# A drain written out by hand: eight pieces of an expert's first product, three routing groups, GpSimd for the W2 halves

## The chip, the core and the metric

The kernel runs on one core of a Trainium2 chip. TensorE (PE in the profile; PEld is its weight load), VectorE (DVE), ScalarE (ACT) and GpSimd (POOL) each run their own instruction list in order; SyncE (SP) issues most of the transfers, also in order. The metric is the device time of one execution in microseconds; lower is better.

## The reference, cut to what matters

Chunked attention (chunks of 64, 8 heads of 64) makes 4608 tokens of 512 numbers; each token then passes a mixture of eight experts, if its skip score is positive:

```python
scores = scale * np.matmul(q_c, k_c.transpose(0, 1, 2, 4, 3))
scores = scores - np.max(scores, axis=-1, keepdims=True)
attn = np.exp(scores)
attn = attn / (np.sum(attn, axis=-1, keepdims=True) + 1e-09)
out = np.matmul(attn, v_c)
...
do_compute = x @ w_skip > 0
e_idx = np.argmax(xc @ w_gate, axis=1)
for e in range(E):
    mask = e_idx == e
    h = np.maximum(xc[mask] @ w1[e], 0.0)
    y[mask] = gate_w[mask, None] * (h @ w2[e])
out[do_compute] = xc + y
```

`w1` is 8 x 512 x 1024, `w2` 8 x 1024 x 512.

## The kernel before, in words

**Tile loop (L605).** The tokens are 36 tiles of 128 (NT = 36). Iteration i works on several tiles at once: scores of tile i+1 (L211), their row maximum on VectorE (L216), its subtraction (L222), the exponential on ScalarE (L226), transposes of the probabilities (L233), product with v (L248), division into x (L258), transposes of x (L279), x split into two float16 parts `xh` (L290 on ScalarE, L292 and L293 on GpSimd; for the last three tiles L286 on ScalarE and L287 on VectorE), nine logits by eight small matmuls (L306, L307), and their reduction `lg` (L316). The loop runs to i = NT + 3, so its last four iterations hold only the tail of the last tiles.

**Routing.** Tiles are routed in groups, `GS = (14, 9, 7, 6)`. When a group's last logits are there, the generator `route` (L323) gives out small steps: kind "d" is VectorE work (maximum, exponent, comparisons `eh`, gate; later `ad`, `rank`, `bi`, `sl`, `key`, `ohb` and one one-hot `oh` per tile, L393, with a product `rv` on GpSimd, L392), kind "p" TensorE work (rank matmuls L363 to L366, record matmuls L410). `run_route` takes a few steps per iteration, up to a budget. After group 2 the first three blocks of 128 tokens of the first expert are known; they are gathered by GpSimd (L467), transposed and split into `xt0` (`early_xt`, L480 to L482).

**Weights.** The first expert's weights come in 16 halves (L453), W1 halves first. Each is split into two float16 parts: the high one on ScalarE (L459), the low one on GpSimd (L463, L464) or on VectorE (L461). The staging tiles `wst` have 8 buffers, which the next expert's loads (L573, four chunks of two halves ahead) share.

**Pieces.** `piece()` (L594) is one of eight chunks of the first product of those 384 tokens: 12 matmuls of 128x384 (L488) into one bank of an `sp` tile of two banks. `evac()` moves a finished one to `ht0`: L492 on ScalarE, L493 on VectorE. After the last routing group come the remaining gathers and the second product `y` (L517), with which the expert phase begins; from there on units of blocks follow each other.

**What sets the order.** The code is recorded in the order in which it is written, and each engine runs its part in order. A tile's buffer is written again once its readers are done, so a piece recorded after an `evac()` of the other bank of its `sp` tile waits for that `evac()`. The pools of the expert phase (`ps_h`, `ps_y`, `ps_x`) take the PSUM banks of the loop's pools, and `bpool` takes SBUF of the loop's pool, x tiles included.

Of the kernel before, what the change touches and what calls it, by code (L numbers as in the profile page):

```python
# [18 lines left out]
P = 128  # L19
# [4 lines left out]
DM = H * D  # L24
# [13 lines left out]
GS = (14, 9, 7, 6)  # L38
# [10 lines left out]
W_TILES = (23, 24, 25, 26, 27, 28, 29, 30, 33, 33, 34, 34, 35, 35, 36, 36)  # L49
# [8 lines left out]
EARLY_AT = {EARLY_I: 0, EARLY_I + 1: 1, EARLY_I + 2: 2}  # L58
# [39 lines left out]
def moe_attention_kernel(ctx: ExitStack, tc: tile.TileContext, q: bass.AP, k: bass.AP, v: bass.AP, cst: bass.AP, wall: bass.AP, out: bass.AP):  # L98
# [167 lines left out]
    def stores(i):  # L266
        if 0 <= i - 3 < STORED:
            store(i - 3)
        elif STORED <= i - 3 < NT:
            held.append(i - 3)  # L270
        for _ in range(4 if i > NT - 4 else 0):
            if held:
                store(held.pop(0))

    def pe_xtrans(t):
        x = T[t].pop("x")
        xt = ps_p.tile([P, KC, P], F32, name="xt")
        for j in range(KC):
            nc.tensor.transpose(xt[:, j, :], x[:, j * P:(j + 1) * P], ident)  # L279
        T[t]["xt"] = xt  # L280
# [42 lines left out]
    def route(g):  # L323
# [66 lines left out]
        for i in range(n):  # L390
            yield "d", 200
            nc.gpsimd.tensor_tensor(rv[:, i], ohb[:, i].unsqueeze(1).to_broadcast([P, 4, NB]), vt[:, i, :].unsqueeze(2).to_broadcast([P, 4, NB]), op=ALU.mult)  # L392
# [212 lines left out]
    for i in range(-1, NT + 4):  # L605
# [7 lines left out]
        if i > NT:  # L613
            piece()
# [14 lines left out]
        run_route("d", 900 if i < NT - 1 else 1500)  # L629
        if i in EARLY_AT:  # L630
            early_xt(EARLY_AT[i], xt_bank if i < NT else sp_bank)
# [5 lines left out]
        if w_pend and (len(w_pend) > 1 or W_TILES[FC - 1] < i < W_TILES[FC]):  # L637
            if i < W_TILES[FC]:
                conv_half()
# [6 lines left out]
        if i >= NT:  # L646
            for eng in (nc.vector, nc.gpsimd):
                if w_pend:
                    conv_half(eng)
            evac()  # L650
        if i == NT:
            piece()
            piece()
# [3 lines left out]
    while routes:  # L657
        host.clear()
        run_route("w", 1)
        piece()  # L660
        run_route("p", 1)
        run_route("rd", 1 << 30)
        evac()
# [3 lines left out]
    while todo or evs:  # L667
        evac()
        piece()
# [4 lines left out]
    ps_h = ctx.enter_context(tc.tile_pool(name="ps_h", bufs=3, space=PSUM))  # L674
    ps_y = ctx.enter_context(tc.tile_pool(name="ps_y", bufs=3, space=PSUM))
    ps_x = ctx.enter_context(tc.tile_pool(name="ps_x", bufs=2, space=PSUM))
# [202 lines left out]
```

## Time and profile before

| | us |
|---|---|
| three runs: median (lowest to highest) | 386.1 (384.02 to 386.74) |
| the profiled execution | 388.72 |
| its span, first to last instruction | 387.0 |

The profiled execution is 2.6 us above the median of the runs, and 1.7 us of it lie outside its span. Times in the rows count from the span's start. The profile has a page (busy shares, a strip of 40 slices, the chain of work that ended last) and answers about stretches of the trace. In a timeline row, the first number is the start and the second the duration; "x12" is the number of instructions merged, and "[1.49 <-DVE ht L493]" is idle time of the engine before them with what ended it.

### The profile page before, as it was taken

Reading aid. Unit: us, or ns where it says so; the run is one execution under the profiler, and the core shown is the slowest. Engines: PE = TensorE matmul, PEld = TensorE weight load, DVE = VectorE, ACT = ScalarE, POOL = GpSimd, SP = SyncE. Lnnn points to the kernel's source line nnn. Section 1 sums busy time; section 2 is a strip of 40 time slices with the busy share of each in tenths; the row PEclk is TensorE's granted clock in tenths of the full one; section 3 lists DMA queues with packets and bytes.
Section 4 is the critical chain, followed back from the end, with each engine's and each line's share of the span. In section 5 each row is a group of like instructions: output and inputs, shape, how many; then the busy total and the mean of one; then the engine's idle time right before and its main releaser. Section 6 shows DMA issues by size and latency. Waiting matters only on the chain.

```text
span 387.0 us, 11298 instructions
## 1 busy us (share of the span) xinstructions
PE 328.2 (85%) x4544; PEld 230.0 (59%) x4544; DVE 250.7 (65%) x575; ACT 164.9 (43%) x336; POOL 148.0 (38%) x200
## 2 busy tenths in 40 slices
PE   6777777788776796767699999899999999999992
PEld 3666766677675674433346554476575665859570
DVE  1555545699679668136555599978597686876520
ACT  3344343445654342221514475445465454654320
POOL 5155444478899844034522002512411324011110
PEclk9999989999999876886999999999999999999998
DMA  8999798899988940222547067776747867665000
GB/s 274 392 368 326 242 331 258 274 304 319 337 262 278 323 163 29 81 75 90 142 176 219 3 216 250 238 254 218 249 149 221 269 208 251 206 201 184 29 24 26
DMA packets 42472, 81.83 MB, mean 211 GB/s; under 512 B 5150, under 2 KB 5150, under 8 KB 42416
## 3 DMA queue, kind: packets, MB, share of 16 engines
q1 hardware_dynamic: 39168, 71.47, 55.7%
q0 software_dynamic: 3104, 9.33, 7.9%
q8 instruction: 37, 0.61, 0.7%
q10 hardware_dynamic: 144, 0.26, 0.2%
q14 instruction: 19, 0.16, 0.1%
HBM read 67.01 MB, written 14.17 MB: 210 GB/s over the span
## 4 chain that ended last, share of the span: by engine, by line
PE 69%; DVE 14%; issue 7%; ACT 5%; DMA 3%; POOLq 0%; POOL 0%; ACTq 0%; DVEq 0%
PE y L517 25%; PE hp L488 19%; PE sp L488 5%; PE sp L211 4%; PE xt L279 4%; PE pv L248 4%; DVE oh L393 3%; ACT xs L290 3%; DMA qk<-in_k 2%; PE xq L480 2%; PE xt L306 2%; DVE mx L216 1%; PE pt L233 1%; DVE ht L493 1%; PE sp L222 1%
## 5 line engine op out<-in xcount | busy, mean ns | idle before, releaser
L517 PE MATMUL y<-wset,ht 128*128 128x512 f16 (+7 forms) x552 | 101.9, 379 | 1.2 <-DVE ht L493 1.2
L488 PEld LDWEIGHTS <-wset 128*128 128x128 f16 x864 | 76.0, 101 | 36.4 <-issue 18.4
L488 PE MATMUL hp<-xt,wset 128*128 128x288 f16 (+6 forms) x768 | 81.1, 267 | 1.7 <-DVE ht L493 1.1
L467 POOL DMA_INDIRECT out<-yo,reci x22 | 24.5, 1111 | 146.4 <-DVE yo L527 125.2
L517 PEld LDWEIGHTS <-ht 128*128 128x128 f16 (+7 forms) x552 | 45.7, 101 | 47.7 <-issue 3.4
L691 DVE SCALAR_TENSOR_TENSOR wset<-wst,wset 128x512 f16<-128x512 f32 x112 | 71.5, 683 | 1.4 <-ACT wset L690 0.8
L690 ACT ACTIVATE wset<-wst 128x512 f16<-128x512 f32 x112 | 63.0, 621 | 2.6 <-DMA wst<-in_wall 2.6
L492 ACT ACTIVATE ht<-hp 128x288 f16<-128x288 f32 (+6 forms) x64 | 23.4, 371 | 50.2 <-PE hp L488 49.6
L290 ACT ACTIVATE xs<-xt 128x512 f32<-128x512 f32 x33 | 19.7, 596 | 58.8 <-PE xt L279 57.0
L216 DVE TENSOR_REDUCE mx<-sp 128x8 bf16<-128x512 f32 x36 | 24.7, 687 | 25.5 <-PE sp L211 23.9
L493 DVE SCALAR_TENSOR_TENSOR ht<-hp,ht 128x288 f16<-128x288 f32 (+6 forms) x64 | 25.3, 405 | 23.3 <-ACT ht L492 22.3
L293 POOL TENSOR_TENSOR xh<-xs,xh 128x512 f16<-128x512 f32 x33 | 38.2, 1158 | 2.6
L292 POOL CAST xh<-xs 128x512 f16<-128x512 f32 x33 | 20.4, 617 | 45.3 <-ACT xs L290 45.1
L248 PE MATMUL pv<-v,pts 64*64 64x65 f32 x1152 | 28.6, 229 | 9.5 <-issue 9.0
L211 PE MATMUL sp<-qk 64*64 64x64 f32 x1152 | 27.1, 230 | 6.1 <-issue 4.7
L248 PEld LDWEIGHTS pv<-v,pts 64*64 64x64 f32 x1152 | 23.8, 142 | 11.4 <-issue 10.9
L488 PE MATMUL sp<-xt,wset 128*128 128x384 f16 x96 | 23.6, 418 | 7.1 <-DVE ht L493 6.3
L481 ACT ACTIVATE xt<-xq 128x512 f16<-128x512 f32 (+7 forms) x19 | 9.6, 509 | 42.3 <-PE xq L480 42.3
L279 PE MATMUL xt<-ident,x 128*128 128x128 f32 x144 | 24.9, 297 | 2.8 <-DVE xt L482 1.8
L467 POOL DMA_INDIRECT xg<-out,reci x22 | 24.2, 1101 | 7.3 <-issue 5.2
L211 PEld LDWEIGHTS sp<-qk 64*64 64x64 f32 x1152 | 21.5, 139 | 9.2 <-issue 7.7
L226 ACT ACTIVATE px<-sp 128x512 f32<-128x512 f32 x36 | 21.6, 600 | 11.4 <-PE sp L222 11.3
(118 smaller groups left out, 389.2 us busy)
## 6 DMA issues: line engine op xcount, KB each, us to landing
wst<-in_wall SPq DMA_DIRECT2D x128, 256.0 KB
v<-in_v SPq DMA_DIRECT2D x36, 260.0 KB
qk<-in_q SPq DMA_DIRECT2D x36, 256.0 KB
out<-x SPq DMA_DIRECT2D x36, 256.0 KB
qk<-in_k SPq DMA_DIRECT2D x35, 256.0 KB
xg<-out,reci POOLq DMA_INDIRECT x22, 4.5
out<-yo,reci POOLq DMA_INDIRECT x22, 4.6
qk<-in_k ACTq DMA_DIRECT2D x1, 256.0 KB
```

Of the source, the lines that this page charges most:

```text
L211: nc.tensor.matmul(sp[halves[a], c, j * CH:(j + 1) * CH], qk[halves[c], 0, w], qk[halves[c], 1, w], start=(j == 0), stop=False, skip_group ...
L216: nc.vector.tensor_reduce(mx, T[t]["sp"][:, :, :KC * CH].rearrange("p c (j s) -> p c j s", s=CH), axis=AX.X, op=ALU.max, negate=True)
L248: nc.tensor.matmul(pv[halves[c], jj, m * VW:(m + 1) * VW], pt[halves[jj], c * 2 + jp, halves[a]], vv[halves[jj], c * KC + m, :], start=(m ...
L279: nc.tensor.transpose(xt[:, j, :], x[:, j * P:(j + 1) * P], ident)
L290: nc.scalar.activation(xs, T[t].pop("xt"), AF.Copy, scale=SX)
L293: nc.gpsimd.tensor_tensor(xh[:, 1], xs, xh[:, 0], op=ALU.subtract)
L467: ins = nc.gpsimd.indirect_dma_start(**kw)
L488: nc.tensor.matmul(hp, w[:, a, fc, j * P:(j + 1) * P], xt[:, b, j, :n], start=(m == 0), stop=(m == 11))
L493: nc.vector.scalar_tensor_tensor(ht[:, 1, fc, :n], hp, 0.0, ht[:, 0, fc, :n], op0=ALU.max, op1=ALU.subtract)
L517: nc.tensor.matmul(y[c * P // cg:c * P // cg + n], ht[:, a, fc, o:o + n], w[:, b, fc, P * KC:], start=(f == 0 and m == 0), stop=(f == fw - ...
L690: nc.scalar.activation(w[:, 0, fc, r], st[part], AF.Copy, scale=SW)
L691: nc.vector.scalar_tensor_tensor(w[:, 1, fc, r], st[part], SW, w[:, 0, fc, r], op0=ALU.mult, op1=ALU.subtract)
```

## The change

The loop ends at i = NT - 1. What its last four iterations held, and the `while routes` loop behind it, becomes one straight list of calls. In it the pieces stand one by one: first piece, transposes of tile 34, logits of 33, evacuation, second piece, transposes of 35, logits of 34, evacuation, third piece, logits of 35, the first routing steps, evacuation, fourth piece, rank matmuls, fifth and sixth piece, record matmuls, seventh and eighth. `GS` becomes (14, 9, 13): groups 3 and 4 are one, routed wholly in the list. All W2 halves are split by ScalarE and GpSimd, one per iteration from i = 33 on and the last five in the list; in the last group GpSimd makes `rv` in two instructions of up to seven tiles. W2 loads are issued a little earlier, the third early block and the transposes of the last tiles use `sp` and `pt` banks, the "d" budget is 1100 instead of 900 from i = 27, and `ps_x` is placed before `ps_y`.

```diff
-GS = (14, 9, 7, 6)
+GS = (14, 9, 13)
-W_TILES = (23, 24, 25, 26, 27, 28, 29, 30, 33, 33, 34, 34, 35, 35, 36, 36)
+W_TILES = (23, 24, 25, 26, 27, 28, 29, 30, 32, 33, 33, 34, 34, 34, 35, 35)
-    def pe_xtrans(t):
+    def pe_xtrans(t, bank=None):
...
-            nc.gpsimd.tensor_tensor(rv[:, i], ohb[:, i].unsqueeze(1).to_broadcast([P, 4, NB]), vt[:, i, :].unsqueeze(2).to_broadcast([P, 4, NB]), op=ALU.mult)
+            s = slice(i, i + 1) if g + 1 < NG else slice(i, min(i + 7, n))
+            sv = [P, s.stop - i, 4, NB]
+            if g + 1 < NG or i % 7 == 0:
+                nc.gpsimd.tensor_tensor(rv[:, s], ohb[:, s].unsqueeze(2).to_broadcast(sv), vt[:, s, :].unsqueeze(3).to_broadcast(sv), op=ALU.mult)
...
-    for i in range(-1, NT + 4):
+    for i in range(-1, NT):
...
-        run_route("d", 900 if i < NT - 1 else 1500)
+        run_route("d", 900 if i < sum(GS[:EARLY_G]) + 4 else 1100)
...
-        if w_pend and (len(w_pend) > 1 or W_TILES[FC - 1] < i < W_TILES[FC]):
-            if i < W_TILES[FC]:
-                conv_half()
+        if w_pend and (i > W_TILES[FC] or i < W_TILES[FC] and (len(w_pend) > 1 or i > W_TILES[FC - 1])):
+            conv_half()
...
-        if i >= NT:
-            for eng in (nc.vector, nc.gpsimd):
-                if w_pend:
-                    conv_half(eng)
-            evac()
-        if i == NT:
-            piece()
-            piece()
     feed_load()
-    while routes:
...
+    pe_ptrans(NT - 1)
+    pe_xtrans(NT - 3, sp_bank)
+    ve_norm(NT - 2)
+    ac_pt(NT - 1)
...
+    ac_xs(NT - 3)
+    pe_logits(NT - 4)
+    ve_logits(NT - 4)
+    early_xt(EARLY_B - 1, sp_bank)
+    pe_pv(NT - 1)
+    ve_norm(NT - 1)
+    store(NT - 1)
+    feed_load()
+    conv()
+    piece()
+    pe_xtrans(NT - 2, pt_bank)
+    ac_xs(NT - 2)
+    pe_logits(NT - 3)
+    ve_logits(NT - 3)
+    evac()
+    conv()
+    piece()
+    pe_xtrans(NT - 1, pt_bank)
+    ac_xs(NT - 1)
+    pe_logits(NT - 2)
+    ve_logits(NT - 2)
+    evac()
+    conv()
+    piece()
+    pe_logits(NT - 1)
+    ve_logits(NT - 1)
+    run_route("d", 1 << 30)
+    evac()
+    conv()
+    piece()
+    run_route("p", 1)
+    run_route("rd", 1 << 30)
+    piece()
+    evac()
+    conv()
+    piece()
+    evac()
+    conv()
+    run_route("w", 1)
+    run_route("p", 1)
+    run_route("rd", 1 << 30)
...
     while todo or evs:
+        piece()
         evac()
-        piece()
...
+    ps_x = ctx.enter_context(tc.tile_pool(name="ps_x", bufs=2, space=PSUM))
     ps_y = ctx.enter_context(tc.tile_pool(name="ps_y", bufs=3, space=PSUM))
-    ps_x = ctx.enter_context(tc.tile_pool(name="ps_x", bufs=2, space=PSUM))
```

Lines behind L392 move: L393 is now L396, L459 L462, L492 and L493 L495 and L496, L573 L576.

ScalarE, from the transposes of tile 33 or 34 to the last evacuations, before and now (`xt` out of `sp` is the third early block, `wset` a weight half, `ht` an evacuation, `pe` the routing's exponent):

```order
L286 ACTIVATE xh<-xt 128x512
L238 ACTIVATE pts<-pt 128x512
L481 ACTIVATE xt_153<-sp 128x4x128
L459 ACTIVATE wset<-wst 128x512 x2
L286 ACTIVATE xh<-xt 128x512
L459 ACTIVATE wset<-wst 128x512 x2
L492 ACTIVATE ht_154<-sp 128x384
L286 ACTIVATE xh<-xt 128x512
L459 ACTIVATE wset<-wst 128x512 x2
L492 ACTIVATE ht_154<-sp 128x384
L335 ACTIVATE pe<-ex 128x48
```

```order
L484 ACTIVATE xt_153<-sp 128x4x128
L462 ACTIVATE wset<-wst 128x512
L286 ACTIVATE xh<-pt 128x512
L495 ACTIVATE ht_154<-sp 128x384
L462 ACTIVATE wset<-wst 128x512
L286 ACTIVATE xh<-pt 128x512
L495 ACTIVATE ht_154<-sp 128x384
L462 ACTIVATE wset<-wst 128x512
L335 ACTIVATE pe<-ex 128x104
L495 ACTIVATE ht_154<-sp 128x384
L462 ACTIVATE wset<-wst 128x512
L495 ACTIVATE ht_154<-sp 128x384
```

Each evacuation now stands between the `xh` of two tiles, directly behind its piece, and the halves come singly.

VectorE, the last group's steps behind the rank matmuls, before and now:

```order
L371 TENSOR_TENSOR ad<-xt,eh 128x54
L376 TENSOR_REDUCE rank<-ad 128x6
L379 SCALAR_TENSOR_TENSOR bi<-rank,fixed 128x6
L382 SCALAR_TENSOR_TENSOR sl<-bi,rank 128x6
L384 SCALAR_TENSOR_TENSOR key<-val,bi 128x6
L387 SCALAR_TENSOR_TENSOR ohb<-csb,key 128x132
L393 SCALAR_TENSOR_TENSOR oh<-csb,sl,onesf 128x128 x6
L493 SCALAR_TENSOR_TENSOR ht_154<-sp,ht_154 128x384
L412 TENSOR_TENSOR rec<-rec,xt 128x88
```

```order
L371 TENSOR_TENSOR ad<-xt,eh 128x117
L376 TENSOR_REDUCE rank<-ad 128x13
L379 SCALAR_TENSOR_TENSOR bi<-rank,fixed 128x13
L382 SCALAR_TENSOR_TENSOR sl<-bi,rank 128x13
L384 SCALAR_TENSOR_TENSOR key<-val,bi 128x13
L387 SCALAR_TENSOR_TENSOR ohb<-csb,key 128x286
L396 SCALAR_TENSOR_TENSOR oh<-csb,sl,onesf 128x128 x13
L496 SCALAR_TENSOR_TENSOR ht_154<-sp,ht_154 128x384 x2
L415 TENSOR_TENSOR rec<-rec,xt 128x88
```

Thirteen one-hots instead of six stand ahead of the evacuation, and two evacuations ahead of the record.

SyncE's transfers from the last v tile on, before and now (`wst` by L453 or L456: W2 halves; `out<-x`: stores of x; L573 or L576: the next expert's loads):

```order
L130 DMA v<-in_v 128x520
L453 DMA wst<-in_wall 128x512 x2
L264 DMA out<-x 128x512 x4
L453 DMA wst<-in_wall 128x512 x2
L264 DMA out<-x 128x512 x4
L453 DMA wst<-in_wall 128x512 x2
L264 DMA out<-x 128x512 x2
L453 DMA wst<-in_wall 128x512 x2
L264 DMA out<-x 128x512 x3
L573 DMA wst<-in_wall 128x512 x36
```

```order
L130 DMA v<-in_v 128x520
L456 DMA wst<-in_wall 128x512 x6
L264 DMA out<-x 128x512 x4
L456 DMA wst<-in_wall 128x512 x2
L264 DMA out<-x 128x512 x4
L576 DMA wst<-in_wall 128x512 x8
L264 DMA out<-x 128x512 x5
L576 DMA wst<-in_wall 128x512 x28
```

The last five stores now stand behind eight of the next expert's loads; the eighth of these takes the buffer of the last W2 half.

## Rows read from the trace of the kernel before

**Rows 1.** The page: the span.

```profile
span 387.0 us, 11298 instructions
```

**Rows 2.** Busy time by stretch: start and end, length, then PE, PEld, DVE, ACT, POOL busy (with instructions), granted clock as a share of full speed, DMA share, GB/s.

```profile
110.00:141.50 31.50, 23.56 (x572) 20.55 (x570) 25.31 (x66) 13.36 (x25) 26.50 (x37) 0.84 0.83 273
141.50:152.40 10.90, 6.76 (x122) 5.44 (x115) 9.01 (x32) 4.95 (x9) 4.42 (x12) 0.79 0.14 51
152.40:189.30 36.90, 26.23 (x148) 14.29 (x148) 16.77 (x50) 8.53 (x19) 13.74 (x20) 0.78 0.24 76
189.30:387.00 197.70, 186.97 (x1397) 118.04 (x1396) 135.59 (x251) 90.08 (x194) 42.06 (x38) 0.99 0.56 181
```

**Rows 3.** The chain of work that ended last, in order of time (start, length), from the logits of tile 31 to the first piece.

```profile
142.96 0.17 PE xt L306
144.03 0.82 DVE den L355
148.44 0.70 DVE xh L287
149.75 1.57 DVE oh L393 x6
151.78 0.61 DVE xt L482
152.44 8.81 PE sp L488 x36
```

**Rows 4.** The same chain from the transposes of tile 34 on; the row of `eh` is from the timeline, where a row has line, operation and shapes.

```profile
161.25 0.45 PE xt L279 x4
161.78 0.61 ACT xh L286
162.41 0.70 DVE xh L287
164.16 0.60 DVE wset L461
164.76 0.48 DVE ht L493
165.28 3.63 PE sp L488 x12
171.16 1.97 PE sp L488 x12
173.34 0.19 DVE lg L316
174.72 0.21 DVE L346 SCALAR_TENSOR_TENSOR eh<-csb,val 128x54 f16<-128x54 f32 x1
175.73 0.57 DVE ht L493
176.34 4.00 PE sp L488 x12
180.62 0.23 DVE ad L371
181.58 0.29 DVE ohb L387
181.88 1.98 DVE oh L393 x6
183.86 0.47 DVE ht L493
```

**Rows 5.** Groups of instructions in 152.4 to 189.3 (count, busy us, mean ns, idle before them), and from the timeline the first matmuls of the second product.

```profile
L488 PE MATMUL sp<-xt,wset 128*128 128x384 f16 x96 | 23.6, 418 | 7.1 <-DVE ht L493 6.3 <-DVE xt L482 0.9
189.34 2.97 PE L517 MATMUL y<-wset,ht 128*128 128x512 f16 x13 [1.17 <-DVE ht L493]
```

**Rows 6.** Single microseconds, with the columns of Rows 2.

```profile
146.00:147.00 1.00, 0.00 (x0) 0.00 (x0) 1.00 (x4) 0.00 (x0) 0.72 (x3) 1.00 0.00 0
148.00:149.00 1.00, 0.25 (x2) 0.00 (x0) 0.60 (x2) 0.95 (x2) 0.36 (x2) 0.50 0.09 33
170.00:171.00 1.00, 0.18 (x8) 0.18 (x8) 0.69 (x1) 1.00 (x4) 0.00 (x0) 1.00 0.00 0
```

**Rows 7.** Timeline of VectorE and GpSimd: one-hots and small routing steps beside GpSimd's work.

```profile
119.01 3.18 DVE L393 SCALAR_TENSOR_TENSOR oh<-csb,sl,onesf 128x128 f16<-128x128 f32 x5
123.75 1.16 POOL L464 TENSOR_TENSOR wset<-wst,wset 128x512 f16<-128x512 f32 x1
123.83 1.23 DVE L393 SCALAR_TENSOR_TENSOR oh<-csb,sl,onesf 128x128 f16<-128x128 f32 x1
70.14 1.09 DVE L333 SCALAR_TENSOR_TENSOR ex<-lg,m 128x112 f32<-128x112 f32 x1
182.02 2.03 POOL L392 TENSOR_TENSOR rv<-ohb,vals 128x88 f16<-128x88 f16 x6 [3.96 <-DVE ohb L387]
```

**Rows 8.** Timeline of GpSimd: the split of a tile's x, the first of three early gathers, and the next tile's split.

```profile
129.66 1.15 POOL L293 TENSOR_TENSOR xh<-xs,xh 128x512 f16<-128x512 f32 x1
130.98 1.25 POOL L467 DMA_INDIRECT xg<-out,reci  x1 [0.17 <-DMA out<-x]
134.88 0.63 POOL L292 CAST xh<-xs 128x512 f16<-128x512 f32 x1
```

**Rows 9.** Timeline of TensorE: the transposes of the second unit's tokens.

```profile
200.99 0.44 PE L480 MATMUL xq<-ident,xg 80*128 80x80 f32 x4
```

More of the change, by code (lines that the diff above doesn't have):

```diff
@@ L57 @@
 EARLY_I = NT - 2
-EARLY_AT = {EARLY_I: 0, EARLY_I + 1: 1, EARLY_I + 2: 2}
+EARLY_AT = {EARLY_I: 0, EARLY_I + 1: 1}
 SX = 2.0 ** 6
@@ L270, in stores @@
             held.append(i - 3)
-        for _ in range(4 if i > NT - 4 else 0):
+        for _ in range(4 if i > NT - 3 else 0):
             if held:
                 store(held.pop(0))
-    def pe_xtrans(t):
+    def pe_xtrans(t, bank=None):
         x = T[t].pop("x")
-        xt = ps_p.tile([P, KC, P], F32, name="xt")
+        xt = bank().rearrange("p (k s) -> p k s", k=KC) if bank else ps_p.tile([P, KC, P], F32, name="xt")
         for j in range(KC):
@@ L603, in evac, with pt_bank @@
             l1_ev(ht0, N0, *evs.pop(0))
-    for i in range(-1, NT + 4):
+    def pt_bank():
+        return ps_p.tile([P, DM], F32, name="pt")
+    for i in range(-1, NT):
         host.clear()
@@ L612, in moe_attention_kernel @@
         run_route("w", 1)
-        if i > NT:
-            piece()
         on(pe_xtrans, i - 3)
@@ L628, in moe_attention_kernel @@
         run_route("r", 1)
-        run_route("d", 900 if i < NT - 1 else 1500)
+        run_route("d", 900 if i < sum(GS[:EARLY_G]) + 4 else 1100)
         if i in EARLY_AT:
-            early_xt(EARLY_AT[i], xt_bank if i < NT else sp_bank)
+            early_xt(EARLY_AT[i], xt_bank)
         on(pe_scores, i + 1)
@@ L645, in moe_attention_kernel, with conv @@
         early_fetch()
-        if i >= NT:
-            for eng in (nc.vector, nc.gpsimd):
-                if w_pend:
-                    conv_half(eng)
-            evac()
-        if i == NT:
-            piece()
-            piece()
-    feed_load()
-    while routes:
[L658 to L663, printed above, removed]
+    feed_load()
+    def conv():
+        if w_pend:
+            conv_half()
+    host.clear()
+    pe_ptrans(NT - 1)
+    pe_xtrans(NT - 3, sp_bank)
+    ve_norm(NT - 2)
+    ac_pt(NT - 1)
+    while held:
+        store(held.pop(0))
+    store(NT - 3)
+    store(NT - 2)
+    ac_xs(NT - 3)
[39 more added lines that the diff above has]
+    run_route("rd", 1 << 30)
     for m in range(NB):
@@ L667, in moe_attention_kernel @@
     while todo or evs:
+        piece()
         evac()
-        piece()
+    while w_pend:
+        conv()
     apool.__exit__(None, None, None)
```

## The prediction

> **What bounds the kernel now.** I read the page first: a span of 387.0 us [rows 1]. Then the busy time by stretch. The expert phase, from 189.3 us on, is TensorE's: 187.0 of 197.7 us busy at a granted clock of 0.99. The drain, 152.4 to 189.3, keeps it busy for 26.2 of 36.9 us at a clock of 0.78, and the stretch before it for 6.8 of 10.9 at 0.79 [rows 2]. The change leaves every engine's order from the second product on as it is, so it can gain only before 189.3, and what it gains there the end gets.
>
> Third, the chain of waits. Between the logits of tile 31 at 142.96 and the first piece at 152.44 lies VectorE's routing of group 3, `den` 0.82, one-hots 1.57, and behind them the third early block's split [rows 3]. In the drain each piece is followed by a turn: transposes, ScalarE 0.61, VectorE 0.70, an evacuation 0.48, and only then the next piece, at 165.28 [rows 4]. The groups say the same: the 96 matmuls of the eight pieces take 23.6 us and wait 7.1, nearly all for `ht` on VectorE [rows 5].
>
> Fourth, the clock. One piece takes 1.97 us at 2.4 GHz and 4.00 at 1.2 GHz [rows 4]. Eight at full clock would be 15.8, so the low clock costs 23.6 - 15.8 = 7.8 us. After TensorE sat idle through 146 to 147 the clock was 0.50 at 148; after the shorter gap before 170.8 it stayed at 1.00 [rows 6].
>
> **The change, part by part.**
>
> *Loop, tiles 28 to 35: 0 taken.* Here GpSimd is busy for 26.5 of 31.5 us [rows 2]. Removed from VectorE are the steps of group 3. Added on GpSimd are three W2 splits, about 1.8 us each (1.16 of it in [rows 7]). The early gathers come one iteration earlier, so one more tile's `xh` waits behind them: in the trace the next `xh` started 3.9 us after the first gather [rows 8], and the logits need it. But up to tile 30's `xh` GpSimd's list holds the same instructions in both kernels, only in another order, and it has no slack, so that tile's logits come when they came. Behind it, tiles 31 to 35 gain what VectorE loses and lose what GpSimd gains. Bounds: 2.5 us better, by `den` and one-hots [rows 3]; 3 us worse, by three splits at 1.8 less the 15% of its time that GpSimd had free.
>
> *First piece: -3.4.* Group 3's steps no longer stand ahead of it. From 142.96: logits and their reduction 0.6; then the second early block, the product with v, two sets of transposes, four groups of about 0.6 (the nearest row is 0.45 for one [rows 4]) to 146.0; the turn of tile 33, 0.61 + 0.70 and gaps [rows 4], to 147.5; the third early block, which shares that tile's `sp` buffer and so waits for the turn, 0.6 for its transposes and 0.6 on ScalarE, to about 149.0. Before: 152.44 [rows 3]. Bounds -5 and -2, as that turn is hidden or the clock is low.
>
> *First piece to second product: 36.9 becomes 33.3, so -3.6.* The path now:
> - four pieces at 1.97: 7.9;
> - behind the first, 0.6 for transposes and a turn: the second piece lies in the other bank of the same tile and waits for the first's evacuation. 0.61 + 0.70 + 0.57 [rows 4], `lg` and gaps 0.4: 2.9 in all. The order does not remove this wait;
> - behind the second, transposes and logits, 0.9, no wait;
> - behind the third, logits, `lg` and the routing steps up to `eh`, 174.93 - 173.34 = 1.6, and an evacuation 0.57 for the same reason [rows 4]: with the logits 2.4. I add 0.6, since `ex`, one of these steps, took 1.09 in a stretch where GpSimd was at work [rows 7], and now GpSimd splits W2 here: 3.0;
> - behind the fourth, rank matmuls 0.5, `ad` to `ohb` 1.25 before (180.62 to 181.87 [rows 4]), 1.6 with 13 tiles, then thirteen one-hots and an evacuation 0.57, after which the seventh piece may start. Fifth and sixth piece fit beside this at either clock;
> - two pieces, 3.9.
>
> The one-hots have three prices: 1.57 / 6 = 0.26 alone [rows 3], 1.98 / 6 = 0.33 beside `rv` [rows 4, 7], 3.18 / 5 = 0.64 beside GpSimd's float32 work [rows 7]. So thirteen cost 3.4 to 8.3. Beside them now run `rv`, which cost 2.03 for six tiles [rows 7] and in two instructions perhaps 2.6 for thirteen, and the last W2 split, 1.9: 4.5 us in which seven pass at 0.64, then six at 0.26: 6.1. So this leg is 0.5 + 1.6 + 6.1 + 0.6 = 8.8.
>
> One row shows why it may be more: the one-hot that started at 123.83 ended at 125.06, just after GpSimd's subtraction of 123.75 to 124.91 [rows 7]. The Trainium skill (SBUF — State Buffer, Who interferes with whom) has the rule: a VectorE instruction with two SBUF inputs and a GpSimd one that reads SBUF share a read port, and whoever starts first holds it for the whole instruction. By it the thirteen cost 3.4 + 4.5 = 7.9, and the total would come out 1.8 us later.
>
> Sum at full clock: 7.9 + 2.9 + 0.9 + 3.0 + 8.8 + 3.9 = 27.4. The low clock: six pieces lie on the path instead of eight, 7.8 x 6 / 8 = 5.9. The waits of 2.3, 2.1 and, before the seventh piece, some 4 us are as long as those after which it fell before [rows 6]. So 33.3. Bounds: 27.4, no low clock; 27.4 + 6 x 2.03 + 2.2 = 42, all six at 4.00 and the one-hots at 8.3.
>
> *Start of the second product.* It waited 1.17 us for the last evacuation [rows 5], because its bank was that piece's. With `ps_y` last among the pools its bank is another; this is in the sum, which ends with the eighth piece.
>
> *W2 halves on GpSimd alone: 0 beyond the above.* VectorE loses four splits, of which one stood on the chain, 0.60 ahead of the evacuation at 164.76 [rows 4]. The last half is needed by the second product's seventh of eight chunks, some 4.5 us in, and is split before it begins.
>
> *SyncE: 0.* Five stores now wait behind eight loads, the last of which needs the buffer of the last W2 half, some 22 us into the drain. Behind the stores wait the gathers and the first split of the next expert, whose buffer lies over x. The gathers are first needed 11.65 us after the second product's start (200.99 against 189.34 [rows 5, 9]); five stores of 256 KB at the 181 GB/s of the expert phase [rows 2] take 7 us. So they land near 178, 4 us before the second product in my sum and 15 before the gathers are needed; without that cover ScalarE and VectorE would stall by the excess.
>
> **Sum.** Profiled execution 388.7 - 3.4 - 3.6 = 381.7. It was 2.6 above the median of the runs, 386.1; from the median 7.0 off gives 379.1. I forecast **379 us**. The bound that this measurement can tell is about 1%, 3.9 us.
>
> **The rivals.**
> - *The clock stays up (20%).* The pieces stand closer, so that the gaps are like the one before 170.8, after which it held [rows 6]. Then 5.9 more is saved: 373. For it: the longest wait of the old order is gone. Against it: three waits over 2 us remain.
> - *The gain is eaten (23%).* The loop slips by 3 us behind the gathers and the W2 splits, or the one-hots cost 8 and more and the clock is lost again before the seventh piece: 383 to 388, taken as 385. For it: GpSimd has little left in the stretch before [rows 2], and the first and third piece of a tile pair are still followed by a wait. This includes that the list does not hide what it is written to hide.
> - *Slower (7%).* VectorE's routing of thirteen tiles meets GpSimd's splits all along: nine small steps at the price of `ex` in the crowded stretch, 0.8 more each, +7; thirteen one-hots at 0.64, +2; TensorE waits so long that all six pieces run at 1.2 GHz, +6. Together +15, less the 7 forecast: 394. It decides once these exceed 11 us. For it: six one-hots cost 1.6 alone and 3.8 crowded [rows 3, 7]. Against: between its halves GpSimd waits for ScalarE, and while `ad` to `ohb` run it has nothing to do.
>
> The forecast, a drain 4 to 10 us shorter (376 to 382), has 50%. Its own range leaves out half; from 372 to 386 it takes in two thirds of the first rival and three quarters of the second: 0.50 + 0.13 + 0.17 = 0.80. Faster by over 1% (below 382.2): forecast and first rival and a little of the second, 0.71. Slower by over 1% (above 390.0): 0.07. Within: 0.22.
>
> **What would show it.** In the profile after: the first piece some 3 us earlier after the same logits; between first and second piece, and third and fourth, TensorE waiting for `ht` on VectorE, 2 to 3 us; none between fifth and sixth; one-hots at 6 us with GpSimd's `rv` and split beside them; the second product directly behind the eighth piece, near 182; a granted clock between 0.75 and 0.9 in the drain; an expert phase of 197.7 us. I am wrong if the expert phase is longer (stores and gathers late), if tile 35's scores come more than 3 us later (GpSimd), or if the clock is 1.00 throughout the drain.

## The result, and the profile after

| | before | changed |
|---|---|---|
| median of 14 runs each, us | 387.31 (384.02 to 396.87) | 381.15 (377.56 to 387.83) |
| ratio, 95% interval | | 0.984 (0.9802 to 0.9877) |
| the profiled execution; its span | 388.72; 387.0 | 381.37; 379.6 |

The ratio's interval means 4.7 to 7.6 us off the 386.1 that the forecast started from; the forecast was 7. Ratios leave out the executions in the chip's slower state, as the one profiled for `y_bank_back` was, and medians don't, so that some medians below lie further apart than their ratios.

The busy time of the changed kernel by stretch, cut at the transposes of tile 32, the first piece and the second product (columns as in [rows 2]):

```profile
110.00:142.96 32.96, 23.74 (x595) 20.78 (x593) 22.58 (x61) 15.42 (x28) 29.18 (x41) 0.86 0.76 257
142.96:150.17 7.21, 5.42 (x107) 4.58 (x107) 4.14 (x12) 4.42 (x9) 5.08 (x6) 1.00 0.16 50
150.17:181.85 31.68, 24.79 (x155) 14.29 (x155) 17.94 (x50) 6.63 (x14) 12.48 (x15) 0.84 0.26 90
181.85:379.60 197.75, 186.97 (x1399) 117.97 (x1396) 136.80 (x253) 91.86 (x197) 44.93 (x41) 0.99 0.57 183
```

The expert phase is that of before (197.75 against 197.70); all of the gain lies ahead of it. The drain went from 36.9 to 31.7 us, at a clock of 0.84 instead of 0.78, the first piece came 2.3 us earlier, and GpSimd is now busy for 29.2 of 33 us ahead of it. The pieces in the timeline of TensorE (start, length, count, and in brackets the idle time before the first and what ended it):

```profile
150.17 2.19 PE L491 MATMUL sp<-xt,wset 128*128 128x384 f16 x12
154.81 2.11 PE L491 MATMUL sp<-xt,wset 128*128 128x384 f16 x12 [1.84 <-DVE ht L496]
157.40 2.11 PE L491 MATMUL sp<-xt,wset 128*128 128x384 f16 x12
162.65 3.28 PE L491 MATMUL sp<-xt,wset 128*128 128x384 f16 x12 [2.96 <-DVE ht L496]
166.57 4.20 PE L491 MATMUL sp<-xt,wset 128*128 128x384 f16 x24
172.96 2.36 PE L413 MATMUL xt<-rv,oh 128*128 128x88 f16 x9 [1.03 <-DVE oh L396]
175.53 6.49 PE L491 MATMUL sp<-xt,wset 128*128 128x384 f16 x24 [0.21 <-DVE ht L496]
181.85 0.38 PE L520 MATMUL y<-wset,ht 128*128 128x512 f16 x1
```

Read from the top: piece 2 and piece 4 wait for the evacuation of the piece before them, piece 3, 5 and 6 for nothing. Then TensorE waits for one-hots, and pieces 7 and 8 take 6.49 us, where 5 and 6 take 4.20: the clock. The second product starts without a wait. In single microseconds the clock shows where it was lost (columns as above):

```profile
165.00:166.00 1.00, 1.00 (x6) 0.57 (x5) 0.00 (x0) 0.03 (x1) 0.00 (x0) 0.50 0.57 213
172.00:173.00 1.00, 0.04 (x1) 0.04 (x1) 1.00 (x2) 0.00 (x0) 0.76 (x1) 1.00 0.00 0
174.00:175.00 1.00, 0.97 (x5) 0.42 (x4) 1.00 (x5) 0.00 (x0) 0.00 (x0) 0.50 0.82 219
180.00:181.00 1.00, 1.00 (x6) 0.55 (x5) 0.00 (x0) 0.00 (x0) 0.11 (x1) 0.75 0.00 0
```

It is 0.50 (1.2 GHz) at 165, a little behind the wait of 2.96, and from 174 to 180 behind the gaps in which TensorE waits for one-hots, the longest of them 1.03. VectorE's thirteen one-hots, and GpSimd's work beside them, in the timeline:

```profile
166.80 0.28 DVE L371 TENSOR_TENSOR ad<-xt,eh 128x117 f32<-128x117 f32 x1 [3.55 <-PE xt L366]
168.31 6.70 DVE L396 SCALAR_TENSOR_TENSOR oh<-csb,sl,onesf 128x128 f16<-128x128 f32 x13
168.53 2.29 POOL L395 TENSOR_TENSOR rv<-ohb,vals 128x616 f16<-128x616 f16 x2 [3.91 <-DVE ohb L387]
170.90 0.62 POOL L466 TENSOR_SCALAR wst<-wst 128x512 f32<-128x512 f32 x1
171.60 1.15 POOL L467 TENSOR_TENSOR wset<-wst,wset 128x512 f16<-128x512 f32 x1
```

### The profile page after: what moved, and what is told of

It is laid out like the page before. It is cut to its first block, busy times and chain, and to the rows that moved or that the text cites. A ratio compares the mean times of both kernels' runs of the same rounds, so it can differ in the third digit from the quotient of the medians.

```text
span 379.6 us, 11266 instructions
## 1 busy us (share of the span) xinstructions
PE 327.1 (86%) x4543; PEld 230.5 (61%) x4543; DVE 245.6 (65%) x552; ACT 165.3 (44%) x335; POOL 152.2 (40%) x195
## 4 chain that ended last, share of the span: by engine, by line
PE 70%; DVE 15%; issue 6%; ACT 4%; POOL 1%; DMA 1%; POOLq 0%; ACTq 0%; DVEq 0%
PE y L520 25%; PE hp L491 19%; PE sp L211 5%; DVE oh L396 5%; PE sp L491 4%; PE xt L279 4%; PE pv L248 4%; ACT xs L290 3%; PE xq L483 2%; DVE mx L216 2%; PE pt L233 2%; PE xt L306 2%; PE xt L162 1%; PE sp L222 1%; DVE x L258 1%
## 5 line engine op out<-in xcount | busy, mean ns | idle before, releaser
L491 PEld LDWEIGHTS <-wset 128*128 128x128 f16 x864 | 74.9, 99 | 32.2 <-issue 12.8
L290 ACT ACTIVATE xs<-xt 128x512 f32<-128x512 f32 x33 | 19.7, 596 | 61.3 <-PE xt L279 58.8
L495 ACT ACTIVATE ht<-hp 128x288 f16<-128x288 f32 (+6 forms) x64 | 23.6, 370 | 49.7 <-PE hp L491 49.4
L496 DVE SCALAR_TENSOR_TENSOR ht<-hp,ht 128x288 f16<-128x288 f32 (+6 forms) x64 | 25.2, 404 | 22.6 <-ACT ht L495 21.5
L292 POOL CAST xh<-xs 128x512 f16<-128x512 f32 x33 | 20.4, 617 | 42.3 <-ACT xs L290 42.2
L248 PE MATMUL pv<-v,pts 64*64 64x65 f32 x1152 | 27.4, 228 | 8.5 <-issue 8.1
L258 DVE TENSOR_TENSOR x<-pv,rr 128x512 f32<-128x512 f32 x36 | 24.9, 691 | 1.2
L233 PE MATMUL pt<-ident,px 128*128 128x128 f32 x144 | 23.7, 291 | 1.4 <-ACT xs L290 1.4
```

The source lines that it names most:

```text
L233: nc.tensor.transpose(pt[:, j, :], px[:, j * P:(j + 1) * P], ident)
L248: nc.tensor.matmul(pv[halves[c], jj, m * VW:(m + 1) * VW], pt[halves[jj], c * 2 + jp, halves[a]], vv[halves[jj], c * KC + m, :], start=(m ...
L258: nc.vector.tensor_tensor(x.rearrange("p (g m d) -> p g m d", g=2, m=KC), pv[:, :, :, :D], rr.unsqueeze(3).to_broadcast([P, 2, KC, D]), op ...
L290: nc.scalar.activation(xs, T[t].pop("xt"), AF.Copy, scale=SX)
L491: nc.tensor.matmul(hp, w[:, a, fc, j * P:(j + 1) * P], xt[:, b, j, :n], start=(m == 0), stop=(m == 11))
```

## The experiments

All variants stand beside runs of the kernel before on the same chip; the chips differ between groups of variants. Where a run moved the total by less than its spread, its trace is read by stages: tile 26's maximum (in the loop, ahead of what the change moves) to the first piece; first piece to second product; second product to the end.

| kernel | median, us | ratio to before (95%) | tile 26 to piece 1 | piece 1 to `y` | `y` to end |
|---|---|---|---|---|---|
| before, first trace | 387.31 | | 53.5 | 36.9 | 197.7 |
| before_again | 386.22 (one run) | | 54.1 | 34.0 | 197.6 |
| changed, first trace | 381.15 | 0.984 (0.980 to 0.988) | 50.5 | 31.7 | 197.8 |
| changed_again | 380.02 | 0.988 (0.977 to 0.998) | 50.7 | 29.4 | 199.9 |
| gather_late | 380.19 | 0.989 (0.978 to 1.001) | 47.7 | 31.6 | 197.9 |
| w2_by_vector | 378.37 | 0.982 (0.965 to 1.000) | 51.3 | 30.3 | 197.8 |
| y_bank_back | 385.76 | 0.995 (0.989 to 1.001) | 50.9 | 32.4 | 199.9 |
| four_groups | 376.24 | 0.980 (0.966 to 0.993) | 53.7 | 27.4 | 198.1 |
| evac_first | 376.61 | 0.983 (0.966 to 0.999) | 49.9 | 25.8 | 198.1 |
| own_banks | 376.09 | 0.972 (0.942 to 1.003) | 50.4 | 25.8 | 199.9 |
| banks_and_evac | 372.13 | 0.967 (0.958 to 0.975) | 49.5 | 21.1 | 197.8 |
| all_three | 374.16 | 0.971 (0.962 to 0.980) | 51.8 | 21.0 | 199.2 |
| split_last | 373.94 | 0.970 (0.955 to 0.985) | 50.3 | 19.7 | 201.6 |
| four_on_both | 372.57 | 0.970 (0.961 to 0.980) | 54.3 | 18.6 | 197.6 |

### The same kernels again

Both unedited kernels got a second trace, to see how much of a difference is the run's.

> The changed kernel itself, unedited, to stand beside the variants of this group on the same chip. In the first group the loop's 15th to 18th tile took up to 3 us more or less from kernel to kernel although all had the same instructions there. Theory (that is run to run): the first piece lies 44 to 45.5 us behind the 27th tile's max as before (150.17 - 105.4 = 44.8), the first piece to the second product takes 31 to 32.5 us, the expert phase 197.7, and the time is 377 to 382 as the loop falls. Rival (the variants' faster loop was theirs): 380.5 to 382 in every run.

> The kernel before, unedited, for a second trace of its loop and drain. Theory (the change moved nothing in the loop beyond 1 us; what differed is run to run): from the 27th tile's max to the 35th's 36 to 37.5 us, as in the first trace (36.6) and near the seven traces of the changed loop so far (37.0 to 38.9); first piece to second product 36 to 38. Rival (the loop slips behind the early gathers): 36.6 or less again, so that the changed loop's mean of 37.5 is a loss of 1 us.

Run to run it is: the two changed traces agree to 0.2 us from tile 26 to the first piece, but one loop is 3 us ahead of the other at tile 26 (96.74 against 99.69), the drains differ by 2.3 and the expert phases by 2.1. In changed_again the clock fell in the drain at 172 to 175, and again from 237 to 240; in the first trace it fell in the drain at 163 to 167 and 174 to 180, and then not before 375. The drains expected were 31 to 32.5 and 36 to 38, and both were missed: 29.4 and 34.0. From tile 27 to tile 35 before_again took 35.1, so the theory's 36 to 37.5 was missed too; but that trace had lost 1.7 us just ahead of tile 27, and from tile 26 it took 42.6, the first trace 42.3. The eight traces with the changed loop and three groups (without gather_late and y_bank_back) took 42.1 to 44.5, in the mean 43.2: the loop slipped by about 0.7 us, less than these traces differ among themselves.

### What was merged: three routing groups

```diff
-GS = (14, 9, 13)
+GS = (14, 9, 7, 6)
...
+    for kind in ("w", "p", "rd", "w", "p", "rd"):
+        run_route(kind, 1 << 30)
     early_xt(EARLY_B - 1, sp_bank)
```

> The changed kernel with group 3 (seven tiles) routed by itself again, before the first piece, and only six tiles at the end. Theory (the saving ahead of the first piece comes from the merged groups, and is paid back in part behind the fourth piece): the first piece starts 2.5 to 3.5 us later than 150.17, near 153; from the rank matmuls to the last one-hot it takes 3.5 to 5 us less than the 8.2 of the changed kernel; the second product starts between 180 and 182.5, the time is 380 to 382, within 0.4% of the changed kernel. Rival 1 (merging the groups is where the 6 us come from): 384 to 387. Rival 2 (thirteen one-hots in a row are what keeps the gain small, since TensorE goes idle and loses its clock there): 376 to 379.

TensorE ahead of the first piece, and the last pieces, in the trace of four_groups:

```profile
146.46 0.85 PE L413 MATMUL xt<-rv,oh 128*128 128x88 f16 x7 [1.38 <-DVE lg L316]
149.21 3.85 PE L491 MATMUL sp<-xt,wset 128*128 128x384 f16 x12
172.72 4.06 PE L491 MATMUL sp<-xt,wset 128*128 128x384 f16 x24 [0.25 <-DVE ht L496]
176.62 3.62 PE L520 MATMUL y<-wset,ht 128*128 128x512 f16 x16
```

The seven tiles' record matmuls stand ahead of the piece again, and from tile 35's maximum to the first piece it takes 10.07 us instead of 7.35: 2.7 us later, as the theory says (the start itself, 149.21, is early because the whole loop was). The drain is 4.3 us shorter than in the changed kernel's first trace, 2.0 shorter than in the second: pieces 7 and 8 ran at full clock. So **merging the groups moved 2.7 us out of the stretch before the first piece and put 2.0 to 4.3 into the drain.** The time agrees with rival 2 (376 to 379); the ratio's interval does not tell it from the changed kernel's. With its old groups this kernel has the stretch ahead of the first piece of the kernel before (53.7 against 53.5 and 54.1), and a drain of 27.4 against 36.9 and 34.0. So in these traces the gain over the kernel before comes from the list and the small edits beside it, not from the merged groups.

### W2 halves by GpSimd or VectorE

```diff
 def conv():
     if w_pend:
-        conv_half()
+        conv_half(nc.vector)
```

> The changed kernel with the W2 splits of the hand-ordered list (five halves) made by VectorE in one instruction each, GpSimd only in the loop. Theory (VectorE's splits stand on the chain, each 0.57 us between an evacuation and the next step, and GpSimd's cost little): the evacuations that the second and fourth piece wait for come as now, but the steps behind them come 0.6 us later each; the thirteen one-hots fall from 6.6 us to about 5 as only rv stands beside them; net 0 to 1.5 us slower, 381 to 383. Rival (GpSimd's splits slow VectorE by more than they relieve it): steps and one-hots together 2 us or more faster, 377 to 379.5.

VectorE's one-hots in the trace of w2_by_vector:

```profile
168.99 5.29 DVE L396 SCALAR_TENSOR_TENSOR oh<-csb,sl,onesf 128x128 f16<-128x128 f32 x13
```

They fall from 6.7 to 5.3, while VectorE makes five splits of 0.68 more. The drain, 30.3, lies between the two of the changed kernel, but its mean clock, 0.83, is that of the longer one (31.7 at 0.84, against 29.4 at 0.94). So at an equal clock it is 1.4 us shorter, as much as the one-hots lost; that is one trace, and the times don't tell it from the changed kernel.

### The bank of the second product

```diff
+    ps_y = ctx.enter_context(tc.tile_pool(name="ps_y", bufs=3, space=PSUM))
     ps_x = ctx.enter_context(tc.tile_pool(name="ps_x", bufs=2, space=PSUM))
-    ps_y = ctx.enter_context(tc.tile_pool(name="ps_y", bufs=3, space=PSUM))
```

> The changed kernel with the pools of y and xq in the old order, so that y's first bank is that of the last two pieces again. Theory (the wait of 1.17 us for the last evacuation before the second product was due to that bank): the second product waits 1.0 to 1.3 us for ht on VectorE behind the eighth piece, first piece to second product 1.2 longer, 32.9, and the time 1.2 us (0.3%) more than the changed kernel's. Rival (its weights' and its own evacuations would be waited for anyway): no wait appears, or it is below 0.3 us.

The first matmuls of the second product, in its trace:

```profile
186.63 1.69 PE L520 MATMUL y<-wset,ht 128*128 128x512 f16 x7 [2.29 <-DVE ht L496]
```

The wait is there, and it is 2.29 us, twice the expected: the list records the eighth piece ahead of the seventh's evacuation, and since both lie in one tile, both evacuations come behind the eighth piece (VectorE's at 184.90 and 186.02 in this trace, where the pieces end at 184.3). The ratio rises from 0.988 to 0.995, by 2.7 us, though the two intervals overlap.

### The waits of pieces 2 and 4, and of pieces 7 and 8

Two edits, each alone and then both. `evac_first` takes the fourth piece's evacuation ahead of the routing steps, and pieces 7 and 8 ahead of the record matmuls (these two moves were not tried apart); `own_banks` puts pieces 2 and 4 into the banks of the product with v, which are free by then, and with `spare.clear()` gives pieces 1, 3 and 5 a fresh `sp` tile each.

```diff
     piece()
     run_route("p", 1)
+    evac()
     run_route("rd", 1 << 30)
     piece()
-    evac()
     conv()
+    piece()
+    piece()
     piece()
     evac()
```

> The changed kernel with the fourth piece's evacuation before the steps ad to the one-hots, and the seventh and eighth piece before the record matmuls. Theory (pieces 7 and 8 are late because they stand behind an evacuation and record matmuls that both wait for thirteen one-hots, 6.6 us in which TensorE has one piece to do and loses its clock): pieces 5 to 8 run without a wait from 166.6 on, at 2.4 GHz, and end near 175; the one-hots end about 0.6 later, near 175.7; the record matmuls end there, and the second product starts at 176 to 177 instead of 181.85. Time 375 to 376.5, 5 us less. Rival 1 (the clock falls all the same, since the waits before piece 4 cause it): pieces at 4 us each, the second product at 181 to 183, 380.5 to 382. Rival 2 (what is late next: the second product then waits for the last W2 half or for evacuations 5 to 8 on VectorE behind the one-hots): the start comes at 176 to 178 but the expert phase is 2 to 4 us longer, 378 to 380.

In its trace pieces 5 to 8 are one block, with the record matmuls behind it:

```profile
162.45 8.56 PE L491 MATMUL sp<-xt,wset 128*128 128x384 f16 x48
170.84 1.07 PE L413 MATMUL xt<-rv,oh 128*128 128x88 f16 x13
172.32 1.02 PE L520 MATMUL y<-wset,ht 128*128 128x512 f16 x4 [0.40 <-DVE rec L415]
```

Four pieces in 8.56 us; the clock is low only at 160 to 163, behind the wait that is still there before piece 4. The drain is 25.8, as the theory has it (26 from 150.17 to 176), and the expert phase 198.1.

```diff
+    def pv_bank():
+        return ps_p.tile([P, 2, DM], F32, name="pv")[:, 0]
+
     def piece():
         if todo:
             fc = todo.pop(0)
-            hp = sp_bank()[:, :N0]
+            if fc < 5:
+                spare.clear()
+            hp = (pv_bank if fc in (1, 3) else sp_bank)()[:, :N0]
```

> The changed kernel with the second and fourth piece in the banks of the product with v, which are free by then, so that they don't wait for the evacuation of the piece before; the order is kept. Theory (the waits of 1.84 and 2.96 us before pieces 2 and 4 are due to the shared tile, and what is hidden behind them is shorter): piece 2 starts about 1.8 us earlier, piece 4 right behind the logits of tile 35 but then the rank matmuls wait for eh instead; of the 4.8 us about 2.5 to 3.5 are gained at the rank matmuls, and the pieces from the fourth on may hold the clock: the second product at 178 to 179.5, 377 to 379. Rival 1 (the same VectorE chain, x to xh to logits to lg to eh, sets the rank matmuls anyway, and TensorE only waits elsewhere): within 1 us of the changed kernel, 380.5 to 381.5. Rival 2 (TensorE packs its work earlier and sits idle longer before the rank matmuls, so that the pieces behind run at 1.2 GHz): 382 to 384.

Its pieces in the timeline of TensorE:

```profile
152.08 2.11 PE L491 MATMUL pv<-xt,wset 128*128 128x384 f16 x12
154.67 2.11 PE L491 MATMUL sp<-xt,wset 128*128 128x384 f16 x12
156.82 2.11 PE L491 MATMUL pv<-xt,wset 128*128 128x384 f16 x12
159.95 4.06 PE L491 MATMUL sp<-xt,wset 128*128 128x384 f16 x24
166.82 2.36 PE L413 MATMUL xt<-rv,oh 128*128 128x88 f16 x9 [1.03 <-DVE oh L396]
168.97 6.36 PE L491 MATMUL sp<-xt,wset 128*128 128x384 f16 x24
```

And one microsecond of it, with the columns of [rows 2]:

```profile
167.00:168.00 1.00, 0.97 (x5) 0.41 (x4) 1.00 (x5) 0.00 (x0) 0.00 (x0) 0.50 0.32 72
```

Both waits of 1.84 and 2.96 are gone, and nearly all of it is gained, not the 2.5 to 3.5 expected: piece 5 starts 10.5 us behind piece 1, in changed_again, where the clock held so far, 14.9 (162.39 - 147.46). The drain is 25.8 although the clock is 0.50 from 167 to 173, behind the gap for the one-hots. Rival 1, that VectorE's chain sets the rank matmuls anyway, falls.

> Both edits together: own banks for pieces 2 and 4, and the fourth piece's evacuation and pieces 7 and 8 ahead of the thirteen one-hots and the record matmuls. Theory: the two gains are of different waits and add: first piece to second product 25.8 in either alone, 31.7 with neither, so 20 to 21 with both. What is late next: the gathers of the second block stand behind five stores on SyncE, which wait for the loads before them and these for GpSimd's last W2 split; they were issued at 167 to 170 in both variants and one gather was waited for 1.7 us; so the expert phase becomes 200 to 203 instead of 197.7, and the time 371 to 374 (with the loop of the changed kernel's profile). Rival 1 (the gains overlap, since VectorE's steps to the last one-hot set the end in both): drain 23.5 to 25, 374 to 377. Rival 2 (the stores are no limit): expert phase 198, 368 to 371.

The stretches of its drain and expert phase:

```profile
148.53:169.59 21.06, 19.77 (x156) 12.38 (x155) 17.11 (x44) 6.21 (x14) 11.58 (x14) 1.00 0.26 86
169.59:367.40 197.81, 186.99 (x1397) 117.94 (x1397) 138.03 (x260) 92.22 (x198) 45.61 (x41) 0.99 0.58 188
```

Its last pieces, in the timeline of TensorE:

```profile
159.07 7.96 PE L491 MATMUL sp<-xt,wset 128*128 128x384 f16 x48
166.87 2.31 PE L413 MATMUL xt<-rv,oh 128*128 128x88 f16 x13
169.59 2.76 PE L520 MATMUL y<-wset,ht 128*128 128x512 f16 x12 [0.41 <-DVE rec L415]
```

The drain is 21.1, TensorE busy for 19.8 of it, at a clock of 1.00 throughout. This version beats both kernels: 0.967 of the time before (0.958 to 0.975), against 0.984 (0.980 to 0.988). The theory's second half fell: the stores behind the loads cost nothing (rival 2 for the expert phase), which is 197.8.

### What is late next

> As the kernel with both edits, and the five stores ahead of the eight weight loads on SyncE (the loop's last call that feeds loads is left out; the list has one behind the stores). Theory: the stores land by 160, the gathers are done when they are wanted, the expert phase is 197.7 to 198.5, the drain 20 to 21 as without it: 2 to 4 us faster than both edits alone, 368 to 371 with the loop of the changed kernel's profile. Rival 1 (the stores were no limit): equal to both edits alone within 1 us. Rival 2 (the loads behind the stores come late, and the second expert's weights are not split in time): the expert phase is 200 or more all the same, the waits now for wset on ScalarE or VectorE.

The edit removes the `feed_load()` at the loop's end from banks_and_evac. The timeline of all_three: SyncE's queue, and the first gather of the next block on GpSimd:

```profile
129.94 22.23 SPq L264 DMA_DIRECT2D out<-x  x9
152.27 40.77 SPq L576 DMA_DIRECT2D wst<-in_wall  x20
...
171.60 1.06 POOL L470 DMA_INDIRECT xg<-out,reci  x1 [3.36 <-DVE recg L435]
```

The stores went early as meant, and the gather now waits for its indices instead of the stores, but nothing was gained (rival 1 for the drain): its expert phase is 1.4 us longer, the clock being 0.50 from 172 to 175, though TensorE was busy from the second product's start on. The gap before it was of the same length in banks_and_evac, 0.41, and there the clock held.

The next edit, against banks_and_evac, holds the last split back:

```diff
     piece()
-    conv()
     piece()
     piece()
     piece()
     evac()
-    conv()
     run_route("w", 1)
     run_route("p", 1)
     run_route("rd", 1 << 30)
+    evac()
+    conv()
```

> Both edits together (own banks, evacuation first), and the last W2 half handed to GpSimd only when the thirteen one-hots are done. Theory (a one-hot that meets a GpSimd instruction with two tensor inputs waits until that ends; one of the thirteen took 1.33 us beside the last subtraction of 1.15, while those beside a one-input GpSimd instruction took 0.34): the thirteen take 5.3 instead of 6.7 us, as in the run with W2 by VectorE, the record matmuls end 1.3 earlier, and the second product starts 19.6 to 20 us behind the first piece instead of 21.06; the split ends before the second product wants it; 1.2 us (0.3%) less. Rival 1 (rv's two instructions are what slows the one-hots): 6.4 to 6.7 and no gain. Rival 2 (the last half comes late): the second product waits 0.5 to 2 us in its sixth or seventh chunk, no gain.

The timeline of its trace: the one-hots, the last split on GpSimd, the eight loads and the five stores on SyncE, the first gather, and the transposes that waited for it:

```profile
163.97 5.29 DVE L396 SCALAR_TENSOR_TENSOR oh<-csb,sl,onesf 128x128 f16<-128x128 f32 x13
170.85 0.62 POOL L466 TENSOR_SCALAR wst<-wst 128x512 f32<-128x512 f32 x1 [4.37 <-ACT wset L462]
140.05 33.01 SPq L576 DMA_DIRECT2D wst<-in_wall  x8
173.16 2.83 SPq L264 DMA_DIRECT2D out<-x  x5
179.81 1.06 POOL L470 DMA_INDIRECT xg<-out,reci  x1 [7.10 <-DMA out<-x]
183.85 0.80 PE L483 MATMUL xq<-ident,xg 80*128 80x80 f32 x4 [2.09 <-DMA xg<-out,reci]
```

The one-hots take 5.29 as expected and the drain 19.65, 1.4 less. But the last load of the eight waits for the buffer of the last half, the stores for that load, the gathers for the stores: counted from the first piece, the first gather moves from 25.3 us (173.85 in banks_and_evac) to 29.5 (179.81). TensorE waits 2.09 for it, loses the clock from 184 to 187, and the expert phase is 201.6. Here SyncE's queue, which cost nothing so far, is the bound, and the gain is lost at the end of its chain. (Late split and early stores together were not tried.)

> Both edits together, and group 3 (seven tiles) routed by itself again before the first piece. With both edits TensorE is busy for 19.8 of the 21.1 us of the drain, so the thirteen one-hots lie beside pieces and cost little. Theory: the first piece comes 2.5 to 3.5 us later against the tile before it (from the transposes of tile 32 to the first piece 9.5 to 10.5 instead of 7.2), the drain gets only 0.5 to 1.5 us shorter, 19.5 to 20.5; net 1.5 to 2.5 us slower than both edits alone, 373.5 to 375. Rival (the routing leg still sets the end and the clock, as in the changed kernel, where four groups took 4.3 off the drain for 2.7 ahead of it): the drain falls to 17 to 18, and the time to 370.5 to 371.5.

The edit is that of four_groups on banks_and_evac. From tile 35 to the first piece 10.04 instead of 7.35, drain 18.61 instead of 21.06: together within 0.3 us of nothing, and the times, 372.57 and 372.13, are within their spread. The drain's saving, 2.4, lies between theory and rival: the routing leg still sets the end of the drain, but what fewer one-hots save there is paid ahead of the first piece. So here the number of groups doesn't matter.

### The early gathers

```diff
-        run_route("d", 900 if i < sum(GS[:EARLY_G]) + 4 else 1100)
+        run_route("d", 900 if i < sum(GS[:EARLY_G]) + 4 else 900)
```

> The changed kernel with the old budget for routing steps in the loop, so that the early gathers stand one tile later on GpSimd, as before the change; everything else stays. Theory (the gathers one tile earlier make the logits of tile 29 wait 4.2 us and cost the clock there, about 1 us of which is left at the first piece): from the 27th tile's max to the 35th's 36 to 36.8 us instead of 37.0 to 38.9, first piece 1 us earlier, drain as in the changed kernel, 29 to 32; 379 to 381. Rival 1 (GpSimd has no slack, so that where the gathers stand makes no difference): 37 to 38 and the same time within 0.3%. Rival 2 (the early blocks come late and the first piece waits for their split): the first piece 1 to 2 us later, 381 to 383.

In the trace of the changed kernel, first the gathers on GpSimd and the tile's `xh` behind them, then the logits that wait:

```profile
130.37 1.26 POOL L470 DMA_INDIRECT xg<-out,reci  x1 [0.18 <-DVE ecum L427]
134.27 0.63 POOL L292 CAST xh<-xs 128x512 f16<-128x512 f32 x1
134.98 1.15 POOL L293 TENSOR_TENSOR xh<-xs,xh 128x512 f16<-128x512 f32 x1
134.95 0.18 PE L306 MATMUL xt<-wgs,xh 128*128 128x18 f16 x1 [2.74 <-POOL xh L292]
136.18 0.19 PE L307 MATMUL xt<-wgs,xh 128*128 128x9 f16 x1 [1.05 <-POOL xh L293]
```

With the gathers from 133.90 on instead of 130.37, tile 26 to 35 took 40.3 us, less than any other trace (42.1 to 44.5), and the first piece came 47.7 after tile 26 instead of 50.5, more than the 1 us expected. The times don't show it: 380.19 against 380.02 for the changed kernel, on another chip. That the gathers cost the loop up to 3 us is what one trace says; whether it is worth anything in the time is open.

## Why the prediction was right, and by how much

The forecast was 379 us, 7.0 below the median; the runs gave 381.15 and a ratio that means 6.2. The mechanism is the one forecast: waits of 1.84 and 2.96 us for `ht` ahead of the second and fourth piece, none between the fifth and sixth, a drain at a clock of 0.84, an expert phase unchanged. That the sum came out so close is in part luck, since in the trace the loop lost 1.4 us that the sum didn't have and the clock cost 1.8 less than it had. By its steps:

- **Loop, 0 taken:** the slip was 1.4 us at tile 31's logits (144.38 against 142.96), of which 0.7 was there at tile 26; over the traces about 0.7. The step argued that GpSimd holds the same instructions up to tile 30's `xh` in another order. That order counted: tile 29's `xh` went behind the gathers, and its logits waited 3.8 us. With the gathers late the loop took 40.3 us from tile 26 to 35, 2 less than in the kernel before, so the 0 hides a gain and a loss of 2 to 3 us each (gather_late's one trace).
- **First piece, -3.4:** from tile 31's logits 5.8 us (150.17 - 144.38) instead of 9.5: -3.7. Less the slip of 1.4, -2.3; between the means of two traces each (53.8 and 50.6 from tile 26) -3.2. Four_groups shows that 2.7 of it is group 3, as the step said, and that it is paid back in the drain. The sum's own terms said so: from `ad` on, thirteen tiles at 1.6 + 6.1, where six had taken 1.25 + 1.98.
- **First piece to second product, 27.4 at full clock:** 31.68, of which the clock is 4.1 (half of the work at 163.4 to 166.6 and at 175.5 to 180.5), so 27.6. Piece by piece, start to start: 4.64 (forecast 1.97 + 2.9), 2.59 (1.97 + 0.9), 5.25 (1.97 + 3.0); fourth piece and rank matmuls 4.15, of which 1.7 is clock (2.47); `ad` to the last one-hot 8.2 (7.7); the evacuation 0.5 (0.6); pieces 7 and 8 6.32, of which 2.4 is clock (3.9).
- **The low clock, 5.9:** the term that was mis-sized. It took 4.1 us in the first trace, where pieces 1, 2, 3, 5 and 6 ran at full clock, and about 1.7 in the second (half of 172 to 175). The step spread it over all six pieces on the path; it fell on pieces behind a wait, the fourth and the last two in the first trace and the last two in the second. The 36.9 that it was taken from was one execution's, too: before_again's drain is 34.0. Between the means of two traces each the drain lost 4.9 us, where the forecast had 3.6.
- **One-hots, 6.1:** 6.7. By the rule of the Trainium skill (SBUF — State Buffer, Who interferes with whom), that whoever has the shared port holds it for the whole instruction, the prediction had 7.9. The trace agrees with the rule and shows where the sum was too high: each of the four GpSimd instructions held one one-hot for about its own length, and that one-hot's own 0.26 lies inside (their records are 0.34 long and overlap; one starts every 0.26). So 2.29 + 0.62 + 1.15 + 9 x 0.26 = 6.4, and 6.7 measured; without the split 5.29.

The one-hots of the changed kernel in short stretches of the trace (count, shortest, median and longest in ns, first and last start in us; each row holds all that ran in its stretch):

```profile
L396 DVE SCALAR_TENSOR_TENSOR oh<-csb,sl,onesf x2: 767/960/1153, 169.8 to 170.9; 128x128 f16<-128x128 f32 x2
L396 DVE SCALAR_TENSOR_TENSOR oh<-csb,sl,onesf x2: 767/1045/1323, 170.9 to 171.6; 128x128 f16<-128x128 f32 x2
L396 DVE SCALAR_TENSOR_TENSOR oh<-csb,sl,onesf x11: 337/339/1323, 169.8 to 174.7; 128x128 f16<-128x128 f32 x11
```

The one at 170.9 took 0.77 beside the multiplication of 0.62, the one at 171.6 took 1.32 beside the subtraction of 1.15, and those behind it 0.34. So here the GpSimd multiplication, which has one tensor input, held a one-hot as well; the expectation of split_last, which put 0.34 beside it, was wrong on that point.

- **Second product's bank:** in the sum by its 1.17; with the list and the old bank the wait is 2.29.
- **W2 halves 0, SyncE 0:** no run contradicts the first, and the second held. The stores landed later than the 178 forecast, for the gathers waited for them until 180.89, but the transposes that need them ran at 193.51 without a wait. The cover named there, stores that land early enough, is real: split_last took it away and paid.
- **The rivals:** the clock did not stay up in the changed kernel. In banks_and_evac it did, at 372 us, but there the waits of pieces 2, 4 and 7 were gone as well, so this is not the 373 of that rival. The gain was not eaten, the slower case not near.

## What to carry to other kernels

When a hand-ordered list puts work of one engine between another's steps, look at which buffer each piece takes and where its release stands: pieces in the two halves of one tile were 4.8 us of waits, and an evacuation and record matmuls recorded ahead of the last two pieces, but behind thirteen one-hots, cost another 4 to 6. An idle gap can be paid twice, by itself and by the clock behind it, so closing the last gaps can be worth more than their length. And before moving work later, follow the chain of its buffer: a split held back by 4.3 us moved loads and stores on SyncE, gathers on GpSimd and transposes on TensorE.

## What the hardware showed that was not expected

- The clock falls behind some gaps and not behind others of the same length: in the changed kernel it held behind the wait of 1.84 us and fell behind that of 2.96, in changed_again (waits of 1.83 and 2.97 at the same places) it held behind both; behind a gap of 0.41 it held in banks_and_evac and fell in all_three. Two traces of one kernel differ by 2.3 us in the drain for this alone. The expert phases of 199.9 are the same thing: every trace but two has TensorE waiting 57.8 us behind the second product's start, for 1.27 to 1.85 us; in changed_again, own_banks and y_bank_back (1.80, 1.85, 1.73) the clock fell behind it, in four_groups and evac_first (1.76, 1.70) it held.
- Around tiles 9 to 18, ahead of all that was changed, the loop lost or won several us from run to run (without y_bank_back, tile 8's maximum lies at 30.2 to 32.2 us and tile 14's at 51.5 to 58.0); the DMA engines were 81 to 97% busy from 50 to 68 us in the fourteen traces. What decides it stays open. Between the two traces of the changed kernel it is the largest difference, and the reason why stages of a trace were compared.
